# A new order for the first tiles' attention, joined with reworked token mixing

## Chip, cores and metric

The kernel runs on one core of a Trainium2 chip. The metric is the device time of one execution in microseconds (us). TensorE is called PE in the profile (PEld is its weight load), VectorE is DVE, ScalarE is ACT, GpSimd is POOL, SyncE is SP.

## What is computed

```
attn = softmax(mask(q @ k.T / 8)) @ v            # 4 batches, 8 heads, 576 tokens, 64 per head; window of 64 keys
x    = attn as [4, 576, 512]
xn   = (x - mean) / sqrt(var + 1e-6) * g
x    = x + relu(xn @ wa1) @ wa2                  # 512 -> 2048 -> 512
h    = relu(x.T @ tok1) @ tok2                   # token mixing, 576 -> 256 -> 576, over the tokens
u    = x + h.T
out  = u + relu(u @ wb1) @ wb2                   # 512 -> 1536 -> 512
```

All inputs are fp32. The weights come in as 64-bit words and are turned into fp32 on the chip, and each large product is made of three passes, since each operand is split into a high and a low part (`PASSES` in line 339).

## The kernel before, in words

The 2304 tokens are 18 tiles of 128, in six blocks of three tiles. There are four stages.

**Opening.** Ten matmuls on zeros (line 391) run while the first loads are under way. Then the attention of the first three tiles runs by a list written out by hand, `FIRST` (line 39), one letter and number for each step; the same list sets the order on all engines, since each engine takes its instructions in program order. `S` t makes the scores of tile t on PE (line 181) and takes the mask, the scale and the row maximum on DVE (line 192; half a tile has the number u = 2t or 2t+1). `e` u is the exponential on ACT with the row sum as a second output (line 200). `T` u and `U` u transpose the probabilities on PE (line 213) and copy them out of PSUM on ACT (T, line 217) or on DVE (U, line 215), and they invert the row sums: on POOL in two instructions after a T (lines 219, 220), on DVE in two after a U (lines 222, 223). `V` u multiplies with v on PE (line 265) and by the inverse sum on DVE (line 267). `L` takes mean and variance on DVE (lines 273, 274) and the root on POOL, `N` subtracts the mean on DVE (line 292), `X` and `Y` transpose the result on PE (line 302), `E` c leaves chunk c in `xnt`, its high part by ACT (line 319) and its low part by DVE (line 320). `D` n are n filler matmuls. `k`, `n` and `s` turn a piece of weights: `k` shrinks it on ACT (line 101), `n` narrows it on DVE in two instructions (lines 111 and 114), `s` splits it into a high part (ACT, line 93) and a low part (POOL, line 94) and loads the next piece on ACT's queue (line 427).

The row sums of each half tile have a tile with the tag `sm`, of which there are four buffers (line 190), so the fifth half tile's waits for the first one to be used by `V`. Loads of q, k, v go by SP's queue, first q and k of tile 0, then in the order of `LOADS` (line 48): v0, q and k of tile 1, v1, the gains, q and k of tile 2, v2, and six pieces of weights.

**Blocks a.** Six blocks, each 16 steps f: 12 matmuls of 384 columns (line 353), relu and split (ACT line 342, DVE line 343), and 9 matmuls of 512 columns for step f-2 (line 366). Hooks put the attention of the next block between them. In the first block the hooks also turn two pieces of weights a step: `wnarrow(2)` runs line 111 for both pieces and then line 114 for both, ahead of the relu; `wsplit` comes behind it. In the last block there is no attention, and 13 pieces of the later weights are turned (`b_narrow`, `b_split`).

**Token mixing.** `tok_up` (line 698) runs four times, with two groups of 14 matmuls each: 13 with 128 rows, and as the last one 64 rows of the rest of the tokens, `(w_[r, 1], y[r])` in line 710. `tok_down` (line 717) runs once for each of the 18 tiles, 6 matmuls each (12 for tiles 8 and 17) into one of three PSUM buffers, and DVE adds the result to the tile (line 731). Tiles 0 to 8 come after the first two `tok_up`, 9 to 17 after the other two. Between the steps DVE makes `ut`, the transposed first block, in 16 block transposes (line 328, list `parts`): eight in `tok_up(2)`, eight in `tok_up(3)`. `b_conv` turns one piece of weights: after `tok_up(2)` and after tiles 11, 13 and 15.

**Blocks b.** Six blocks of 12 steps, the same two matmul lines. In the first of them each step turns one piece of weights, so the pieces used last are turned last.

Of the kernel before, what the change touches and what calls it, by code (L numbers as in the profile page):

```python
# [35 lines left out]

FIRST = ("S0 e0 e1 S1 e2 T0 U1 e3 S2 V0 V1 L0 e4 T2 U3 e5 N0 X0 V2 V3 L1 T4 U5 k1 N1 X1 V4 V5 L2 n1 D10 N2 X2 Y0 "
         "k1 D4 s0 n1 E0 E1 E2 E3 s0 k2")  # L40


WARM = 10
# [1 line left out]

LAG = 2

LOADS = ("v0 q1 v1 g0 q2 v2 w6")


def tile_blocks(t):
# [9 lines left out]
def mixer_kernel(ctx, tc, qT, kT, v, g, wa1, wa2, tok1, tok2, wb1, wb2, out):  # L61
# [18 lines left out]
    masks = const.tile([P, 2, 2 * BLK], BF16, name="masks")  # L80
    gsb = const.tile([P, KD], F32, name="gsb")
    mhalf = const.tile([P, 1], F32, name="mhalf")
    mone = const.tile([P, 1], F32, name="mone")
    qkv = const.tile([P, 3, 2, DM], F32, name="qkv")

    def wslot(k, shape, name, dtype=F32R):
# [13 lines left out]
        h_ = raw.rearrange("p (n two) -> p n two", two=2)[:, :, 1].bitcast(F32)  # L100
        nc.scalar.activation(out=h_, in_=h_, func=AF.Prelu, scale=2.0 ** -112, alpha=2.0 ** 32)

    def narrow(pairs, steps=(0, 1)):

        for step in steps:
            for d, r in pairs:
                w = r.rearrange("p (n two) -> p n two", two=2)
                if step == 0:  # L110
                    nc.vector.tensor_scalar(out=d, in0=w[:, :, 0], scalar1=29, scalar2=None,
                                            op0=ALU.logical_shift_right)
                else:
                    nc.vector.scalar_tensor_tensor(out=d, in0=w[:, :, 1], scalar=3, in1=d,
                                                   op0=ALU.logical_shift_left, op1=ALU.bitwise_or)
        return [d.bitcast(F32) for d, _ in pairs]


# [11 lines left out]
    def place_fixed(t):  # L130
        place_in(t, qkv[:, 0, 0], qkv[:, 1], qkv[:, 2])

    def load_qk(t):
        (ba, ia), (bb, ib) = tile_blocks(t)
        ga, gb = ba * NBLK + ia, bb * NBLK + ib
        if ba == bb:
            nc.sync.dma_start(out=Q[t], in_=qT[:, ga:ga + 2, :])
            first = 1 if ia == 0 else 0
            nc.sync.dma_start(out=K[t][:, first:3], in_=kT[:, ga - 1 + first:ga + 2, :])
        else:  # L140
            for s, g_ in ((0, ga), (1, gb)):
                nc.sync.dma_start(out=Q[t][:, s], in_=qT[:, g_, :])
                nc.sync.dma_start(out=K[t][:, 2 * s:2 * s + 2], in_=kT[:, g_ - 1:g_ + 1, :])
# [18 lines left out]
    def att_S(t, lean, first=False):  # L162


        (ba, ia), (bb, _) = tile_blocks(t)
        m_ = masks[:, 1 if ia == 0 else 0]
        wide = [P, NH, 2 * BLK]
        s_ = [ps_acc.tile(wide, F32, tag="acc", name=f"s{2 * t + hh}") if first else
              ps_a.tile(wide, F32, tag="a", name=f"s{2 * t + hh}") for hh in range(2)]
        for h in range(NH):  # L170
            c = slice(h * BLK, (h + 1) * BLK)
            for hh in range(2):
                r = slice(64 * hh, 64 * hh + 64)
                for s in range(2):
                    if s == 0 and ia == 0:

                        k_ = K[t][r, 1:2, c].to_broadcast([64, 2, BLK])
                    else:
                        j = s if ba == bb else 2 * s
                        k_ = K[t][r, j:j + 2, c]  # L180
                    nc.tensor.matmul(s_[hh][64 * s:64 * s + 64, h], lhsT=Q[t][r, s, c], rhs=k_, start=True, stop=True)  # L181
        for hh in range(2):
            u = 2 * t + hh
            if first:
                f_ = scratch[:, u]
            else:
                f_ = sp.tile(wide, F32, tag="s", name=f"f{u}") if lean else whole[t][:, hh]
            probs[u] = f_
            mx = peak[u] = stp.tile([P, NH, 1], F32, tag="mx", name=f"mx{u}")
            norm[u] = stp.tile([P, NH, 1], F32, tag="sm", bufs=4, name=f"sm{u}") if lean else sums[t][:, hh]  # L190
            for h in range(NH):
                nc.vector.tensor_tensor_reduce(out=f_[:, h], in0=s_[hh][:, h], in1=m_, scale=-(D ** -0.5),  # L192
                                               scalar=-2.0 * MASK, op0=ALU.add, op1=ALU.min, accum_out=mx[:, h])
            if lean and not first:
                att_E(u)
# [7 lines left out]
    def att_T(u, first=False, copy=None):  # L203
        f_, sm = probs.pop(u), norm[u]
        if first:
            p_ = ps_h.tile([P, NH, P], F32, tag="h", name=f"pt{u}")
            s_ = hp.tile([P, 2 * N], F32, tag="hT", name=f"pts{u}")[:, 0:NH * P].rearrange("p (h c) -> p h c", h=NH)
        else:
            p_ = ps_a.tile([P, NH, P], F32, tag="a", name=f"pt{u}")
            s_ = sp.tile([P, NH, P], F32, tag="s", name=f"pts{u}")  # L210
        probsT[u] = s_
        for h in range(NH):
            nc.tensor.transpose(p_[:, h, :], f_[:, h, :], ident)
        if copy:
            copy(out=s_, in_=p_)
        else:
            nc.scalar.activation(out=s_, in_=p_, func=AF.Copy)
        if first and not copy:
            nc.gpsimd.tensor_scalar_add(out=sm, in0=sm, scalar1=SM_EPS)
            nc.gpsimd.tensor_tensor(out=sm, in0=sm, in1=mone.unsqueeze(1).to_broadcast([P, NH, 1]), op=ALU.pow)  # L220
        else:
            nc.vector.tensor_scalar_add(out=sm, in0=sm, scalar1=SM_EPS)
            nc.vector.reciprocal(out=sm, in_=sm)

    whole, wholeT, sums = {}, {}, {}

# [8 lines left out]
    def tile_T_part(t, n):  # L235

        if n == 0:
            wholeT[t] = ap.tile([P, 2, NH, P], F32, tag="p", name=f"pts{t}")
        f_, s_ = (x[t].rearrange("p two h c -> p (two h) c") for x in (whole, wholeT))
        a, b = divmod(n, 4)  # L240
        nc.vector.transpose(out=s_[32 * b:32 * b + 32, :, 32 * a:32 * a + 32],  # L241
                            in_=f_[32 * a:32 * a + 32, :, 32 * b:32 * b + 32])
        if n == 15:
            del whole[t]
            for hh in range(2):
                probsT[2 * t + hh] = wholeT[t][:, hh]
            sm = sums.pop(t)
            nc.vector.tensor_scalar_add(out=sm, in0=sm, scalar1=SM_EPS)
            nc.vector.reciprocal(out=sm, in_=sm)

    def tile_PV(t):
        del wholeT[t]
# [132 lines left out]
    with tc.manual_schedule():  # L385
# [10 lines left out]
            place_in(t, qs[:, t - 1, 0], kv_[:, 0], kv_[:, 1])  # L396
        for t in range(TPB):
            new_x(t)
        load_qk(0)

        make_identity(nc, ident)
        for i in (1, 0):
# [9 lines left out]
                nc.gpsimd.memset(m_[0:64, 0], MASK)  # L412
            nc.vector.tensor_copy(out=masks[:, i], in_=m_.rearrange("p s c -> p (s c)"))
        nc.gpsimd.memset(mhalf, -0.5)
        nc.gpsimd.memset(mone, -1.0)
# [50 lines left out]
        def first_X(j, c):  # L466
# [1 line left out]

        fns = {"S": lambda t: att_S(t, True, True), "e": att_E, "D": dummies, "T": lambda u: att_T(u, True),
               "U": lambda u: att_T(u, True, nc.vector.tensor_copy), "V": att_PV,  # L470
               "L": ln_stats, "N": ln_center, "k": wshrink, "n": wnarrow, "s": lambda _: wsplit(False),
               "X": lambda j: [first_X(j, c) for c in range(KD - 1)],
               "Y": lambda _: [first_X(j, KD - 1) for j in range(TPB)], "E": lambda c: evac(c)}
        scratch = xnp.tile([P, 2 * TPB, NH, P], F32, tag="xn", name="scratch")
# [89 lines left out]
                    shrink(x[2][:, 0:2 * x[3]])  # L564
                    x[0] = True

        def b_narrow(n=1):
            b_shrink(n)
            pairs = []
            for _, k, raw, width, parts in ready_b[:n]:  # L570
                tmp = sp.tile([P, DM], U32, tag="s", name=f"tmpb{k}")
                pairs.append((tmp[:, 0:width], raw[:, 0:2 * width]))
                rawb.append(raw)
            narrowed_b.extend((parts, w) for (_, _, _, _, parts), w in zip(ready_b[:n], narrow(pairs)))
# [10 lines left out]
        def b_conv(n=1):  # L585
            for _ in range(n):
                b_narrow()
                b_split()

# [108 lines left out]
        def tok_up(b, between=()):  # L698
            pr, o = divmod(b, 2)
            hb = h1[b] = wslot((12, 13, 14, 13)[b], [P, 2, 2, DM], f"h1_{b}")  # L700
            r = slice(64 * o, 64 * o + 64)
            for tt in range(2):
                ts = slice(tt * P, (tt + 1) * P)
                p_ = ps_h.tile([P, DM], F32, tag="h", name=f"th{b}_{tt}")
# [2 lines left out]
                    w_, y = tw["t1"][:, :, j, ts], ysl(9 * pr + 4 * o + j)  # L707
                    ops += [(w_[:, a], y[:, c]) for a, c in PASSES]
                w_, y = t2[0][:, :, 704 + tt * P:704 + (tt + 1) * P], ysl(9 * pr + 8)[:, o]
                ops += [(w_[:, 0], y), (w_[r, 1], y[r])]  # L710
                for n, (a, b) in enumerate(ops):
                    nc.tensor.matmul(p_, lhsT=a, rhs=b, start=n == 0, stop=n == len(ops) - 1)  # L712
                relu_split(hb[:, tt, 0], hb[:, tt, 1], p_)
# [24 lines left out]
        for t in range(9):  # L738
            tok_down(t)
            if t < 5:  # L740
                new_ys(1, t)
                for y in range(9 + 2 * t, min(11 + 2 * t, 18)):
                    y_split(y, nc.gpsimd if y < 17 else None)
            else:
                y_rest_low(17, t - 5)
        tok_up(2, parts[:8])
        b_conv()
        tok_up(3, parts[8:])
        for c in range(KD):
            split(xnt[:, c, 0], xnt[:, c, 1], ut[:, c], nc.gpsimd)  # L750
        b_shrink()
        for t in range(9, 18):
            tok_down(t)
            if t in (11, 13, 15):
                b_conv()


# [89 lines left out]
```

## Time and profile before

| what | us |
|---|---|
| median of 3 runs (lowest, highest) | 844.45 (843.27, 845.39) |
| the profiled execution, its own time | 844.72 |
| its span, first to last instruction | 842.6 |
| PE busy / DVE / ACT / POOL in the span | 824.9 / 524.5 / 282.0 / 119.5 |
| mean granted clock of PE | 0.996 |

The span is what the trace shows; the 2.1 us beside it are before the first and after the last instruction. Busy time of PE is modelled from pipelined matmuls, so a busy PE need not be at its peak: the question for each stretch is how long the same number of matmuls takes there and elsewhere.

### The profile page before, as it was taken

What the parts mean: (1) busy time and instruction counts of PE and PEld (TensorE: products, weight loads), DVE (VectorE), ACT (ScalarE), POOL (GpSimd) and SP (SyncE); (2) the same over time, 40 slices, a digit from 0 to 9 for tenths busy, and PEclk for the clock granted to TensorE, in tenths of its full rate; (3) what the DMA queues carried; (4) which work ended last, traced back from release to release, by engine and by line L of the source; (5) the groups of instructions that cost most, each with busy time, mean ns of one, the idle gap of its engine ahead of it and who ended that gap; (6) DMA issues with size and microseconds to landing.
All of it is one profiled execution on the core that took longest, in us unless ns stands there. A gap on an engine that the chain in (4) does not pass through costs nothing.

```text
span 842.6 us, 13017 instructions
## 1 busy us (share of the span) xinstructions
PE 824.9 (98%) x5022; PEld 728.8 (86%) x5022; DVE 524.5 (62%) x1313; ACT 282.0 (33%) x759; POOL 119.5 (14%) x141
## 2 busy tenths in 40 slices
PE   6899999999999999999999999999999999999997
PEld 5788888888888888889999876898999999899996
DVE  4899868777787878678557557975343434344211
ACT  5577543334324333442245332432111111111110
POOL 3555510000000000000005341532000000000000
PEclk8999999999999999999999999999999999999999
DMA  9577302102100110211006400531001010010101
GB/s 327 185 264 269 137 32 77 38 26 88 58 26 26 57 57 26 96 58 43 1 0 195 124 1 25 200 100 38 1 0 39 1 38 1 1 37 1 38 1 37
DMA packets 23213, 58.37 MB, mean 69 GB/s; under 512 B 2800, under 2 KB 3568, under 8 KB 23152
## 3 DMA queue, kind: packets, MB, share of 16 engines
q1 hardware_dynamic: 19408, 43.92, 15.7%
q10 hardware_dynamic: 3744, 13.63, 4.5%
q8 instruction: 39, 0.64, 0.3%
q14 instruction: 22, 0.18, 0.1%
HBM read 52.82 MB, written 4.72 MB: 68 GB/s over the span
## 4 chain that ended last, share of the span: by engine, by line
PE 90%; DVE 3%; issue 1%; ACT 1%; POOL 0%; DVEq 0%; ACTq 0%
PE acca L366 23%; PE ha L353 23%; PE hb L353 18%; PE accb L366 17%; PE td L728 2%; PE o L265 2%; PE s L181 2%; PE th L712 1%; DVE ut L328 1%; PE king_offset=None)_1_4976 L712 0%; PE king_offset=None)_1_5121 L712 0%; PE king_offset=None)_1_4941 L712 0%; DVE us L94 0%; DVE xs L731 0%; DVE xs L799 0%
## 5 line engine op out<-in xcount | busy, mean ns | idle before, releaser
L353 PE MATMUL ha<-xnt,wa 128*128 128x384 f32 x1152 | 217.4, 337 | 1.3 <-DVE xnt L320 0.7
L366 PE MATMUL acca<-wa,hTa 128*128 128x512 f32 x864 | 215.9, 396 | 0.0
L353 PEld LDWEIGHTS ha<-xnt,wa 128*128 128x128 f32 x1152 | 203.7, 188 | 9.9 <-DVE xnt L320 1.0
L366 PEld LDWEIGHTS acca<-wa,hTa 128*128 128x128 f32 x864 | 159.0, 188 | 32.5 <-issue 1.7
L366 PE MATMUL accb<-wb,hTb 128*128 128x512 f32 x648 | 159.1, 392 | 0.0
L366 PEld LDWEIGHTS accb<-wb,hTb 128*128 128x128 f32 x648 | 120.7, 188 | 22.5
L343 DVE SCALAR_TENSOR_TENSOR hTb<-hb,hTb 128x384 fp32r<-128x384 f32 x72 | 40.1, 557 | 150.3 <-ACT hTb L342 150.2
L342 ACT ACTIVATE hTb<-hb 128x384 fp32r<-128x384 f32 x72 | 35.4, 492 | 238.6 <-PE hb L353 238.6
L342 ACT ACTIVATE hTa<-ha 128x384 fp32r<-128x384 f32 x96 | 46.6, 486 | 180.4 <-PE ha L353 180.3
L343 DVE SCALAR_TENSOR_TENSOR hTa<-ha,hTa 128x384 fp32r<-128x384 f32 x96 | 53.1, 553 | 85.8 <-ACT hTa L342 84.3
L241 DVE STREAM_TRANSPOSE pts<-f 32x256 f32<-32x256 f32 x192 | 83.6, 436 | 2.8
L353 PE MATMUL hb<-xnt,wb 128*128 128x384 f32 x432 | 80.9, 337 | 1.1 <-POOL wb L94 0.7
L353 PE MATMUL hb<-us,wb 128*128 128x384 f32 x432 | 80.5, 336 | 0.0
L353 PEld LDWEIGHTS hb<-xnt,wb 128*128 128x128 f32 x432 | 76.4, 188 | 4.4 <-POOL wb L94 1.1
L353 PEld LDWEIGHTS hb<-us,wb 128*128 128x128 f32 x432 | 76.5, 188 | 2.6
L336 DVE STREAM_TRANSPOSE xhT<-xh 32x128 f32<-32x128 f32 x192 | 57.9, 302 | 3.1
L200 ACT ACTIVATE f<-f,mx 128x128 f32<-128x128 f32 x120 | 46.5, 389 | 29.4 <-DVE mx L192 29.4
L328 DVE STREAM_TRANSPOSE ut<-xs 32x384 f32<-32x384 f32 x96 | 54.6, 569 | 1.9
L94 POOL TENSOR_TENSOR wa<-tmp,wa 128x512 fp32r<-128x512 f32 x32 | 42.2, 1339 | 34.6 <-ACT wa L93 34.6
L286 POOL TENSOR_SCALAR mv<-mv 128x1 f32<-128x1 f32 x12 | 2.3, 191 | 276.5 <-ACT xhT L285 276.5
L94 POOL TENSOR_TENSOR wb<-tmpb,wb 128x512 fp32r<-128x512 f32 x24 | 32.9, 1380 | 53.9 <-ACT wb L93 53.9
L728 PE MATMUL td<-h,t 128*128 128x512 f32 x120 | 28.6, 395 | 1.6 <-DVE xs L731 1.6
(113 smaller groups left out, 682.4 us busy)
## 6 DMA issues: line engine op xcount, KB each, us to landing
xs<-in_wa ACTq DMA_DIRECT2D x26, 512.0 KB, 4.3
qkv<-in_wb SPq DMA_DIRECT2D x20, 512.0 KB, 4.2
qkv<-in_v SPq DMA_DIRECT2D x28, 256.0 KB, 2.8
out<-xs SPq DMA_DIRECT2D x16, 256.0 KB, 2.1
qkv<-in_kT SPq DMA_DIRECT2D x10, 384.0 KB, 3.3
qkv<-in_qT SPq DMA_DIRECT2D x14, 256.0 KB, 2.7
xs<-in_wa SPq DMA_DIRECT2D x6, 512.0 KB, 7.8
qkv<-in_kT SPq DMA_DIRECT2D x8, 256.0 KB, 3.3
```

The lines of the kernel that those rows point to most:

```text
L94: lo_engine.tensor_tensor(out=dst_lo, in0=src, in1=dst_hi.bitcast(F32), op=ALU.subtract)
L181: nc.tensor.matmul(s_[hh][64 * s:64 * s + 64, h], lhsT=Q[t][r, s, c], rhs=k_, start=True, stop=True)
L200: nc.scalar.activation(out=f_[:, h], in_=f_[:, h], func=AF.Exp, scale=-1.0, bias=mx[:, h], accum_out=sm[:, h])
L241: nc.vector.transpose(out=s_[32 * b:32 * b + 32, :, 32 * a:32 * a + 32], in_=f_[32 * a:32 * a + 32, :, 32 * b:32 * b + 32])
L265: nc.tensor.matmul(o_[r, h], lhsT=p_[:, h, r], rhs=v_[:, s, hh * NH + h, :], start=True, stop=True)
L328: nc.vector.transpose(out=d_[:, :, :, 32 * a:32 * a + 32], in_=s_[:, :, :, 32 * b:32 * b + 32])
L336: nc.vector.transpose(out=uts[t][32 * b:32 * b + 32, :, 32 * a:32 * a + 32], in_=s_)
L342: nc.scalar.activation(out=dst_hi, in_=src, func=AF.Relu)
L343: nc.vector.scalar_tensor_tensor(out=dst_lo, in0=src, scalar=0.0, in1=dst_hi.bitcast(F32), op0=ALU.max, op1=ALU.subtract)
L353: nc.tensor.matmul(h_, lhsT=w[:, a, cs], rhs=src[c][:, b], start=n == 0, stop=n == 3 * KD - 1)
L366: nc.tensor.matmul(acc[j], lhsT=t_[:, a, js], rhs=w[:, 2 + b, :], start=f == 0 and n == 0, stop=f == F - 1 and n == 2)
L728: nc.tensor.matmul(p_, lhsT=t2[tt][:, a, col:col + P], rhs=h1[b][:, tt, c], start=n == 0, stop=n == last)
```

## The change

The opening's list has a new order and no `U5`, `L1` and `N1`: half tile 5 is copied by ACT (`T5`), and tile 1 has its mean and variance taken on ACT in three activations and POOL in two instructions (`l1`). A new step `r` t inverts the sums of a whole tile on DVE in two instructions; neither T nor U inverts any more in the opening, and the sums of the first three tiles lie in a tile of their own each. q and k of tile 1 are loaded ahead of v0, q and k of tile 2 ahead of v1, and the keys of tile 0 go by ACT's queue. `narrow` runs both its instructions for one piece before the next piece's; for the later weights (`b_narrow`) the value between them lies in PSUM instead of SBUF. In the token mixing the last matmul of a group has all 128 rows; two block transposes each run behind tiles 3 and 4; `b_conv` runs inside `tok_up(3)` and once more, behind tile 16.

```diff
-FIRST = ("S0 e0 e1 S1 e2 T0 U1 e3 S2 V0 V1 L0 e4 T2 U3 e5 N0 X0 V2 V3 L1 T4 U5 k1 N1 X1 V4 V5 L2 n1 D10 N2 X2 Y0 "
-         "k1 D4 s0 n1 E0 E1 E2 E3 s0 k2")
+FIRST = ("S0 e0 e1 S1 T0 r0 U1 e2 V0 V1 S2 L0 e3 T2 r1 U3 e4 V2 V3 N0 X0 e5 T4 r2 T5 k1 V4 l1 V5 D6 L2 X1 n1 N2 k1 "
+         "s0 n1 X2 Y0 D4 E0 E1 E2 E3 s0 k2")
-LOADS = ("v0 q1 v1 g0 q2 v2 w6")
+LOADS = ("q1 v0 q2 v1 g0 v2 w6")
-    def narrow(pairs, steps=(0, 1)):
+    def narrow(pairs, pool=None):
+        for d, r in pairs:
+            w, low = r.rearrange("p (n two) -> p n two", two=2), d
+            if pool:
+                low = pool.tile([P, DM], U32, tag="acc" if pool is ps_acc else "a", name="low")[:, 0:d.shape[1]]
+            nc.vector.tensor_scalar(out=low, in0=w[:, :, 0], scalar1=29, scalar2=None, op0=ALU.logical_shift_right)
+            nc.vector.scalar_tensor_tensor(out=d, in0=w[:, :, 1], scalar=3, in1=low,
+                                           op0=ALU.logical_shift_left, op1=ALU.bitwise_or)
...
-            nc.sync.dma_start(out=K[t][:, first:3], in_=kT[:, ga - 1 + first:ga + 2, :])
+            eng.dma_start(out=K[t][:, first:3], in_=kT[:, ga - 1 + first:ga + 2, :])
...
-            norm[u] = stp.tile([P, NH, 1], F32, tag="sm", bufs=4, name=f"sm{u}") if lean else sums[t][:, hh]
+            if first and hh == 0:
+                sums[t] = stp.tile([P, 2, NH, 1], F32, tag="sums", name=f"sums{t}")
+            norm[u] = sums[t][:, hh] if first or not lean else stp.tile([P, NH, 1], F32, tag="sm", bufs=4, name=f"sm{u}")
...
-        if first and not copy:
-            nc.gpsimd.tensor_scalar_add(out=sm, in0=sm, scalar1=SM_EPS)
-            nc.gpsimd.tensor_tensor(out=sm, in0=sm, in1=mone.unsqueeze(1).to_broadcast([P, NH, 1]), op=ALU.pow)
-        else:
-            nc.vector.tensor_scalar_add(out=sm, in0=sm, scalar1=SM_EPS)
-            nc.vector.reciprocal(out=sm, in_=sm)
+        if not first:
+            inverse(sm)
+    def inverse(sm):
+        nc.vector.tensor_scalar_add(out=sm, in0=sm, scalar1=SM_EPS)
+        nc.vector.reciprocal(out=sm, in_=sm)
...
-        load_qk(0)
+        load_qk(0, nc.scalar)
...
-               "L": ln_stats, "N": ln_center, "k": wshrink, "n": wnarrow, "s": lambda _: wsplit(False),
+               "L": ln_stats, "l": ln_scalar, "r": lambda t: inverse(sums.pop(t)), "N": ln_center, "k": wshrink, "n": wnarrow, "s": lambda _: wsplit(False),
...
-        def b_narrow(n=1):
+        def b_narrow(n=1, pool=ps_a):
...
+        def b_conv():
+            b_narrow(1, ps_acc)
+            b_split()
...
-                ops += [(w_[:, 0], y), (w_[r, 1], y[r])]
+                ops += [(w_[:, a], y) for a in range(2)]
...
+            if t in (3, 4):
+                for fn in parts[:2]:
+                    fn()
+                del parts[:2]
         tok_up(2, parts[:8])
-        b_conv()
-        tok_up(3, parts[8:])
+        tok_up(3, [b_conv, *parts[8:], lambda: None, lambda: None, lambda: None])
...
-            if t in (11, 13, 15):
+            if t in (11, 13, 15, 16):
                 b_conv()
```

## Rows read from the trace of the kernel before

**Rows 1.** The page: the chain that ended last, shares of the span by engine.

```profile
PE 90%; DVE 3%; issue 1%; ACT 1%; POOL 0%; DVEq 0%; ACTq 0%
```

**Rows 2.** Stretches: us, then PE, PEld, DVE, ACT, POOL busy; PE clock; DMA share; GB/s.

```profile
7.30:31.46 24.16, 17.04 (x225) 14.61 (x225) 17.17 (x76) 14.44 (x58) 8.13 (x13) 0.86 0.74 275
36.00:60.00 24.00, 22.81 (x194) 19.47 (x193) 23.15 (x49) 17.77 (x44) 14.01 (x11) 1.00 0.78 264
```

**Rows 3.** Groups of DVE, 7.2 to 31.4 us: busy us, mean ns | idle before, releasers.

```profile
L192 DVE CUSTOM_DVE_ANT_0 scratch<-s,masks 128x128 f32<-128x128 f32 x24 | 5.3, 286 | 5.4 <-PE s L181 2.9 <-ACT scratch L200 2.5
L267 DVE TENSOR_TENSOR xs<-o,sm 128x256 f32<-128x256 f32 x6 | 2.4, 422 | 3.1 <-PE o L265 3.1
L114 DVE SCALAR_TENSOR_TENSOR tmp<-xs,tmp 128x512 uint32<-128x512 uint32 x2 | 2.4, 1208 | 0.2
L273 DVE BATCH_NORM_STATS2 st<-xs 128x6 f32<-128x512 f32 x3 | 2.1, 695 | 0.1
L215 DVE COPY pts<-pt 128x512 f32<-128x512 f32 x3 | 2.0, 680 | 0.7 <-PE pt L213 0.7
...
L292 DVE TENSOR_SCALAR xh<-xs,mv 128x512 f32<-128x512 f32 x3 | 1.4, 468 | 0.0
L111 DVE TENSOR_SCALAR tmp<-xs 128x512 uint32<-128x512 uint32 x2 | 0.8, 407 | 0.0
```

**Rows 4.** Timeline of the opening: start us, us, engine, line [idle before <-releaser].

```profile
1.31 4.64 PE L391 MATMUL idle<-zero 128*128 128x512 f32 x10 [1.31 <-POOL zero L388]
...
5.88 1.41 PE L181 MATMUL s<-qkv 64*64 64x128 f32 x32
...
9.71 2.00 PE L181 MATMUL s<-kv,q 64*64 64x128 f32 x32 [2.42 <-DMA kv<-in_kT]
...
16.84 0.40 ACT L200 ACTIVATE scratch<-scratch,mx 128x128 f32<-128x128 f32 x1 [1.24 <-DVE xs L267]
...
31.46 2.18 DVE L320 SCALAR_TENSOR_TENSOR xnt<-tpa,gsb,xnt 128x384 fp32r<-128x384 f32 x4
```

**Rows 5.** Timeline of the token mixing and the start of block b, PE and PEld.

```profile
480.60 2.79 PEld L712 LDWEIGHTS king_offset=None)_1_4941<-ys,t 128*128 128x128 f32 x13 [0.25 <-issue]
...
484.17 2.79 PEld L712 LDWEIGHTS th<-ys,t 128*128 128x128 f32 x13 [0.24 <-issue]
...
491.38 13.94 PE L728 MATMUL td<-h,t 128*128 128x512 f32 x60
...
519.39 4.42 PE L728 MATMUL td<-h,t 128*128 128x512 f32 x18
...
525.24 7.23 PE L728 MATMUL td<-h,t 128*128 128x512 f32 x30 [1.43 <-DVE xs L731]
...
535.54 6.43 PE L353 MATMUL hb<-xnt,wb 128*128 128x384 f32 x36
```

**Rows 6.** Timeline of DVE around the second nine tiles of the token mixing.

```profile
522.13 2.33 DVE L328 STREAM_TRANSPOSE ut<-xs 32x384 f32<-32x384 f32 x4
524.49 1.89 DVE L731 TENSOR_TENSOR xs<-td,xs 128x512 f32<-128x512 f32 x3
...
527.41 1.39 DVE L114 SCALAR_TENSOR_TENSOR tmpb<-qkv,tmpb 128x512 uint32<-128x512 uint32 x1
```

**Rows 7.** Timeline of PE at the last steps of the first block b.

```profile
575.29 2.25 PE L366 MATMUL accb<-wb,hTb 128*128 128x512 f32 x9
...
579.28 2.03 PE L353 MATMUL hb<-xnt,wb 128*128 128x384 f32 x10 [0.73 <-POOL wb L94]
581.14 6.32 PE L366 MATMUL accb<-wb,hTb 128*128 128x512 f32 x27
```

**Rows 8.** Beside each other in the first block a; then the page's group of line 343.

```profile
85.30 2.98 POOL L94 TENSOR_TENSOR wa<-tmp,wa 128x512 fp32r<-128x512 f32 x2 [2.35 <-ACT wa L93]
...
85.61 2.96 DVE L111 TENSOR_SCALAR tmp<-xs 128x512 uint32<-128x512 uint32 x2
...
L343 DVE SCALAR_TENSOR_TENSOR hTa<-ha,hTa 128x384 fp32r<-128x384 f32 x96 | 53.1, 553 | 85.8 <-ACT hTa L342 84.3
```

More of the change, by code (lines that the diff above doesn't have):

```diff
@@ L82, in mixer_kernel @@
     mhalf = const.tile([P, 1], F32, name="mhalf")
-    mone = const.tile([P, 1], F32, name="mone")
     qkv = const.tile([P, 3, 2, DM], F32, name="qkv")
@@ L101, in shrink @@
         nc.scalar.activation(out=h_, in_=h_, func=AF.Prelu, scale=2.0 ** -112, alpha=2.0 ** 32)
-    def narrow(pairs, steps=(0, 1)):
[L107 to L112, printed above, removed]
-                else:
-                    nc.vector.scalar_tensor_tensor(out=d, in0=w[:, :, 1], scalar=3, in1=d,
-                                                   op0=ALU.logical_shift_left, op1=ALU.bitwise_or)
+    def narrow(pairs, pool=None):
[6 more added lines that the diff above has]
+                                           op0=ALU.logical_shift_left, op1=ALU.bitwise_or)
         return [d.bitcast(F32) for d, _ in pairs]
@@ L131, in place_fixed, with load_qk @@
         place_in(t, qkv[:, 0, 0], qkv[:, 1], qkv[:, 2])
-    def load_qk(t):
+    def load_qk(t, eng=nc.sync):
         (ba, ia), (bb, ib) = tile_blocks(t)
@@ L217, in att_T @@
             nc.scalar.activation(out=s_, in_=p_, func=AF.Copy)
-        if first and not copy:
-            nc.gpsimd.tensor_scalar_add(out=sm, in0=sm, scalar1=SM_EPS)
-            nc.gpsimd.tensor_tensor(out=sm, in0=sm, in1=mone.unsqueeze(1).to_broadcast([P, NH, 1]), op=ALU.pow)
-        else:
-            nc.vector.tensor_scalar_add(out=sm, in0=sm, scalar1=SM_EPS)
-            nc.vector.reciprocal(out=sm, in_=sm)
+        if not first:
[3 more added lines that the diff above has]
+        nc.vector.reciprocal(out=sm, in_=sm)
     whole, wholeT, sums = {}, {}, {}
@@ L246, in tile_T_part @@
                 probsT[2 * t + hh] = wholeT[t][:, hh]
-            sm = sums.pop(t)
-            nc.vector.tensor_scalar_add(out=sm, in0=sm, scalar1=SM_EPS)
-            nc.vector.reciprocal(out=sm, in_=sm)
+            inverse(sums.pop(t))
     def tile_PV(t):
@@ L414, in mixer_kernel @@
         nc.gpsimd.memset(mhalf, -0.5)
-        nc.gpsimd.memset(mone, -1.0)
         warm = stp.tile([P, NH, 1], F32, tag="mx", name="warm")[:, 0]
@@ L573, in b_narrow @@
                 rawb.append(raw)
-            narrowed_b.extend((parts, w) for (_, _, _, _, parts), w in zip(ready_b[:n], narrow(pairs)))
+            narrowed_b.extend((parts, w) for (_, _, _, _, parts), w in zip(ready_b[:n], narrow(pairs, pool)))
             del ready_b[:n]
@@ L583, in b_split @@
             del narrowed_b[:]
[L585 to L588, printed above, removed]
+        def b_conv():
+            b_narrow(1, ps_acc)
+            b_split()
         STEPS = ("S0", "T0*7", "T0*8", "T0*1 S1", "V0 T1*3", "T1*8", "T1*5 X0*4", "S2 X0*2", "V1 X0*5", "T2*8",
@@ L700, in tok_up @@
             hb = h1[b] = wslot((12, 13, 14, 13)[b], [P, 2, 2, DM], f"h1_{b}")
-            r = slice(64 * o, 64 * o + 64)
             for tt in range(2):
```

## The prediction, as it was made before the changed kernel ran

> **What bounds it now.** I read the chain of work first: 90% of it is PE [rows 1], so the kernel ends when PE has done its matmuls, and whatever lets PE start its steady work sooner, or closes a hole in it, comes off the end one for one. Then I looked for the places where PE is not in steady work, by the timeline of each stretch, and found three that the change touches. The opening: PE has little to do until DVE writes the low part of the first chunk of `xnt` at 31.46 [rows 4], since the first block needs it. From 7.30 to there DVE is busy 17.17 of 24.16 us, against ACT's 14.44, and PE's granted clock is 0.86 on average: at two levels, 1.2 and 2.4 GHz, some 28% of that stretch ran at the lower one [rows 2]. DVE's idle 7.0 us are waits for the first products, in series with PE and ACT [rows 3]. The token mixing: its groups take longer than their matmuls, and PE stands once for 1.43 us for DVE [rows 5]. The end of the first block b: PE stands for weights that POOL has not yet split [rows 7].
>
> The sum is made against the profiled execution, 844.72 us (span 842.6, and 2.1 around it). The median of the three runs lies 0.27 lower; I don't correct for that. Less than 0.3%, 2.5 us, a measurement of this kernel can't tell from no change.
>
> **The opening.** I take DVE's queue from the end of the first scores, 5.88 + 1.41 = 7.29, since DVE sets the end.
>
> The first scores don't move. They start as the ten warm-up matmuls end, at 1.31 + 4.64 = 5.95 [rows 4], so the keys by a second queue bring nothing there, nor cost anything: SP issues one load less.
>
> The second tile's scores wait 2.42 us for its keys [rows 4], which stood seventh on SP and now stand third. PE then waits for something else: three PSUM buffers hold scores, and the fourth half tile's needs the first one read by DVE, about 1 us after 7.29 (four of the 24 reductions of 0.29). So about 1.4 of 2.42 is gained, and the second reductions run almost at once; v0, behind three loads more, is not wanted until two transposes are copied. The wait of 1.24 for the multiply of V0 before the fifth exponential [rows 4] goes: it was for a buffer of row sums, and each tile has its own now.
>
> Work leaves DVE: one statistic (0.695), one copy (0.680), one subtraction (0.468) [rows 3], 1.8 us. The inverses on DVE stay three pairs; those on POOL go, and were waited for by no one. ACT gets one copy and three activations for tile 1, about 2.7 us at the copy's 0.68 for 512 columns; it was busy 14.44 of 24.16 [rows 2], and it sits beside V4, V5 and the narrowing. The second narrowing's L114 took about 1.7: the mean of the two is 1208 ns, and 0.7 is its length alone by the copy of as many columns, 680 ns [rows 3]. POOL was splitting beside it; now the subtraction N2 and the shrink stand between, and POOL starts later against it: 1.0 gained, or nothing.
>
> Of the 7.0 idle us I count through the new order: 0.4 before the second reductions, 0.4 at U1 and V1, 0.6 before the third ones, 0.3 at V3, 2.3 while X0, T4, T5 and V4 run in series behind N0, 0.9 elsewhere, 4.9 together. That gains 2.1. Sum 1.8 + 1.0 + 2.1 = 4.9. If the clock falls again while T4, T5, V4 and V5 run, they take some 1.3 us more (an estimate: about 2.3 us of work in series, at half the speed, a part of it behind ACT); PE's holes are shorter than before, but V3 and X0 still wait about 2 and 1 us. I take off 0.5 for that: **4.4 us gained**, between 2.0 (the work alone) and 6.0. What comes next, the first block, keeps its order and moves with it: its loads go out from the splits, so none has a fixed time.
>
> **Narrowing.** Both instructions for one piece, then for the next: the same four. The first piece is ready one L111 earlier, and POOL starts sooner, beside the second piece's two. In the first block DVE is the tight engine, 23.15 of 24 us [rows 2]. I take 0, between 1 gained and 3 lost, by L111's 0.407 alone [rows 3] and 2.96 for two beside POOL [rows 8].
>
> **Token groups.** Two groups of 14 matmuls start 484.17 - 480.60 = 3.57 apart by their weight loads; 60 whole matmuls of the same width take 13.94 less 0.16 of overlap, 0.230 each, so 14 would take 3.22 [rows 5]. The 0.35 is the 64-row matmul, before and behind which PE's loads stop. With 128 rows it is like the other 13; the added products come from rows that are loaded anyway. Eight groups: **2.75 gained**, between 2.4 and 2.85.
>
> **Second nine tiles.** From 519.39 to 535.54 they take 16.15 against 13.78 for the same 60 matmuls in the first nine: 2.37 lost, 1.43 in one wait [rows 5]. It begins with DVE's backlog: eight transposes stand ahead of the adds, the last four from 522.13 to 524.46 [rows 6]. Four of the 16 now run behind tiles 3 and 4: each pair is 1.15 there, DVE falls behind by at most about 1 us, and PE has three buffers of 1.38 us, so no hole. Behind `tok_up(3)` the adds start some 2.5 us after the tiles do, ahead of the fourth tile's need at 4.1. Five conversions in place of four now stand in DVE's queue, at twice 0.7 each if PSUM keeps them free of POOL, by the copy out of PSUM [rows 3]. The nearest rows for an instruction with one operand in PSUM are those of line 343: 553 ns in the mean of 96, most of them beside POOL [rows 8]; against that L114 took 1.39 there with both in SBUF [rows 6]. I take the first: DVE then has nine adds of 0.63 (three in 1.89), four conversions of 1.4 and 1.3 of backlog, 12.6 us in 13.8. **2.1 gained**, between 1.0 and 2.4.
>
> The Trainium skill, "SBUF — State Buffer", "Who interferes with whom", says that a DVE instruction with two SBUF inputs, or in a two-port mode, locks GpSimd out or waits for its whole instruction, and that one with at most one SBUF input outside such a mode does neither. By that rule the narrowing through PSUM costs DVE its bare length, and by it the first block's narrowing, which stays in SBUF, is open to the loss in the third rival.
>
> **First block b.** From 575.29 to 581.14 are 5.85 us for 9 and 12 matmuls that take 9 x 0.230 + 12 x 0.174 = 4.16 (0.174 from 36 in 6.43 - 0.16) [rows 5, 7]: 1.7 lost, since the last step's weights were split as it began. With a fifth conversion in the token mixing each piece comes one step, over 4 us, earlier, more than the hole. **1.7 gained**, at worst 0.8. The later narrowings through PSUM in the last block a have slack around them: 0.
>
> **Sum:** 4.4 + 0 + 2.75 + 2.1 + 1.7 = 10.95, so 844.7 - 10.9 = **833.8 us**.
>
> **Rivals.**
> First, the opening gives little: T4, T5, V4 and V5 behind X0 run at the low clock, and three activations of tile 1 on ACT hold the split that the first block needs. For it: 28% at low clock before, and N0 stands at the end of DVE's queue as before. Against it: DVE's work is less whatever PE does. It would gain 1 instead of 4.4: 837.2.
>
> Second, DVE stays behind in the second nine tiles. It was busy nearly all the time there, and gets one conversion more; if L111 and L114 still wait for POOL, each conversion costs some 1.4 more (0.7 for L114, and I put as much for L111), four of them 5.6, and the 2.1 gain turns into a loss of about 2: 838. Against it are line 343's lengths.
>
> Third, slower: the first block. If each step's second L111 or L114 finds POOL in its first split, which the old order kept behind all four, DVE waits out one split of 1.28 (two in 2.98, less a wait for one L111 of 0.41) [rows 8]. In 16 steps that is 20 us. From about 0.4 us a step DVE, with 0.85 us free in 24 [rows 2], holds up PE; were later steps to absorb 6, 14 would stay, 844.7 - 10.9 + 14 = 848. Against it: in the rows shown the old order has both L111 waiting for POOL in many steps, so one collision takes another's place.
>
> That a part does nothing is in the forecast for the second queue; the 64-row matmul can't but go.
>
> **Chances.** The forecast 0.70, the first rival 0.15, the second 0.09, the third 0.06. The range: low, all upper bounds, 6.0 + 1 + 2.85 + 2.4 + 1.7 = 14, to 831; the rivals reach to 838, and both together with 1 us lost in the first block to 840. I give 830.5 to 840. Faster by over 0.3% are the forecast and the first two rivals and a mild third, 0.92; within 0.3% 0.04, where the third takes about as much as is gained; slower 0.04.
>
> **What would show it.** Right: the low part of the first chunk at about 27 us in place of 31.46; no 64-row loads, and token groups 3.2 us apart; the second nine tiles in about 14 us with no wait for line 731; L111 near 0.6 and L114 near 0.69 with POOL beside them; no wait for POOL at the end of the first block b. Wrong: most of the first block's second L111 or L114 over 1.3 us, with PE idle where DVE is tight; the clock at 0.5 around 20 us; or a first block that takes longer than before from its first low part to its last matmul, which would say that the opening's gain was given back.

## The result, and the profile after

| | before | after |
|---|---|---|
| median of 4 runs each, us (lowest, highest) | 844.28 (843.27, 845.39) | 833.48 (833.0, 833.97) |
| the profiled execution, its own time | 844.72 | 833.0 |
| its span | 842.6 | 830.8 |
| mean granted clock of PE | 0.996 | 0.999 |

The ratio is 0.9876 with the interval 0.9863 to 0.9888. The kernel after is faster by 1.24%. The forecast was 833.8; the sum of its terms, 10.95, stands against 10.80 between the medians.

The two profiled executions lie 11.72 us apart, 0.9 more than the medians: the first lies 0.44 above its median, the second 0.48 below. The last section returns to that. To see where the 11.72 lie, take one place of PE's stream that both kernels have, and subtract. The first is the twelve matmuls of the first block's third step, from which PE works steadily.

PE in the timeline of the kernel before: start, us, engine, line, operation, tiles, shapes, count.

```profile
37.38 2.35 PE L353 MATMUL ha<-xnt,wa 128*128 128x384 f32 x12
...
112.94 2.27 PE L353 MATMUL ha<-xnt,wa 128*128 128x384 f32 x12
...
477.14 3.54 PE L712 MATMUL th<-ys,t 128*128 128x512 f32 x14
...
505.15 3.54 PE L712 MATMUL th<-ys,t 128*128 128x512 f32 x14
...
587.30 6.43 PE L353 MATMUL hb<-us,wb 128*128 128x384 f32 x36
```

The same places of the kernel after, and those between them (its lines are numbered a little lower).

```profile
32.91 2.35 PE L350 MATMUL ha<-xnt,wa 128*128 128x384 f32 x12
...
108.69 2.27 PE L350 MATMUL ha<-xnt,wa 128*128 128x384 f32 x12
...
472.88 3.34 PE L706 MATMUL th<-ys,t 128*128 128x512 f32 x14
...
485.57 13.76 PE L722 MATMUL td<-h,t 128*128 128x512 f32 x60
...
499.17 3.33 PE L706 MATMUL th<-ys,t 128*128 128x512 f32 x14
...
511.87 13.76 PE L722 MATMUL td<-h,t 128*128 128x512 f32 x60
...
525.47 6.43 PE L350 MATMUL hb<-xnt,wb 128*128 128x384 f32 x36
...
575.57 6.43 PE L350 MATMUL hb<-us,wb 128*128 128x384 f32 x36
```

| stage | before | after | gained | forecast |
|---|---|---|---|---|
| opening, to the third step | 37.38 | 32.91 | 4.47 | 4.4 |
| first block a, from there to the next block | 75.56 | 75.78 | -0.22 | 0 |
| token groups (64-row matmul) | | | 3.44 | 2.75 |
| second nine tiles, the hole | 16.15 | 13.60 | 2.37 (2.55 less 0.18 counted above) | 2.1 |
| first block b | 51.76 | 50.10 | 1.66 | 1.7 |

The token groups' 3.44 is two things: the two `tok_up` ahead of each nine tiles took 14.24 and take 12.69 and 12.70, and each nine tiles take 13.60. The first nine took 13.77 before, and the second nine would have taken 13.78 without their hole, as they do in the run with 64 rows below. The stages between gave nothing (0.01), and the sum is 11.72.

**The opening** now looks like this. The first row answers to [rows 2], the rest to [rows 4].

Stretch of the kernel after, from 7.30 to the first low part: us, then PE, PEld, DVE, ACT, POOL busy; PE clock; DMA share; GB/s.

```profile
7.30:25.72 18.42, 13.04 (x209) 10.63 (x208) 14.04 (x72) 15.95 (x62) 2.57 (x5) 1.00 0.88 335
```

Timeline of the kernel after.

```profile
5.87 1.30 PE L178 MATMUL s<-qkv 64*64 64x128 f32 x32
...
8.29 1.09 PE L178 MATMUL s<-kv,q 64*64 64x128 f32 x28 [0.91 <-DVE mx L191]
...
20.57 1.17 PE L262 MATMUL o<-kv,pts 128*64 128x64 f32 x32 [0.25 <-ACT pts L216]
...
25.11 0.69 DVE L111 SCALAR_TENSOR_TENSOR tmp<-xs,tmp 128x512 uint32<-128x512 uint32 x1
25.72 2.19 DVE L317 SCALAR_TENSOR_TENSOR xnt<-tpa,gsb,xnt 128x384 fp32r<-128x384 f32 x4
...
26.50 2.54 POOL L93 TENSOR_TENSOR wa<-tmp,wa 128x512 fp32r<-128x512 f32 x2
...
27.84 4.11 PE L350 MATMUL ha<-xnt,wa 128*128 128x384 f32 x22 [0.99 <-POOL wa L93]
```

The reader is to see three things. The first low part starts at 25.72 in place of 31.46, 5.74 earlier. Of these DVE's busy time gives 17.17 - 14.04 = 3.13, and its idle time (24.16 - 17.17) - (18.42 - 14.04) = 2.61. The granted clock is 1.00 all through, where it was 0.86. And the next to be late is POOL: its split of the first weights begins at 26.50, PE waits 0.99 us for it, and of 5.74 us only 4.47 reach the third step.

**The narrowing.** Groups of DVE on the page of the kernel after: busy us, mean ns | idle before. The first two go through PSUM, the last two stay in SBUF.

```profile
L111 DVE SCALAR_TENSOR_TENSOR tmpb<-qkv,low 128x512 uint32<-128x512 uint32 x24 | 16.5, 688 | 2.9
L110 DVE TENSOR_SCALAR low<-qkv 128x512 uint32<-128x512 uint32 x24 | 16.5, 686 | 0.9 <-DMA qkv<-in_tok 0.5 <-DMA qkv<-in_wb 0.3
...
L111 DVE SCALAR_TENSOR_TENSOR tmp<-xs,tmp 128x512 uint32<-128x512 uint32 x32 | 26.9, 840 | 3.9 <-ACT xs L100 0.9
L110 DVE TENSOR_SCALAR tmp<-xs 128x512 uint32<-128x512 uint32 x32 | 22.5, 702 | 0.0
```

### The profile page after: what moved, and what is told of

It reads as the page before. It is cut to its first block, busy times and chain, and to the rows that moved or that the text cites. A ratio compares the mean times of both kernels' runs of the same rounds, so it can differ in the third digit from the quotient of the medians.

```text
span 830.8 us, 12970 instructions
## 1 busy us (share of the span) xinstructions
PE 817.2 (98%) x5014; PEld 726.7 (87%) x5014; DVE 512.4 (62%) x1309; ACT 284.5 (34%) x765; POOL 115.8 (14%) x134
## 4 chain that ended last, share of the span: by engine, by line
PE 93%; DVE 1%; ACT 0%; issue 0%; ACTq 0%; DVEq 0%
PE acca L363 24%; PE ha L350 23%; PE hb L350 18%; PE accb L363 18%; PE td L722 3%; PE o L262 2%; PE s L178 2%; PE th L706 2%; DVE tmp L111 1%; PE king_offset=None)_1_5123 L706 0%; PE king_offset=None)_1_5174 L706 0%; PE king_offset=None)_1_4974 L706 0%; PE king_offset=None)_1_4939 L706 0%; DVE xs L796 0%; DVE tmp L110 0%; PE pt L212 0%
## 5 line engine op out<-in xcount | busy, mean ns | idle before, releaser
L93 POOL TENSOR_TENSOR wa<-tmp,wa 128x512 fp32r<-128x512 f32 x32 | 45.2, 1432 | 30.2 <-ACT wa L92 30.2
L93 POOL TENSOR_TENSOR wb<-tmpb,wb 128x512 fp32r<-128x512 f32 x24 | 31.0, 1297 | 51.8 <-ACT wb L92 51.8
L111 DVE SCALAR_TENSOR_TENSOR tmp<-xs,tmp 128x512 uint32<-128x512 uint32 x32 | 26.9, 840 | 3.9 <-ACT xs L100 0.9
```

The lines of the kernel that those rows point to most:

```text
L93: lo_engine.tensor_tensor(out=dst_lo, in0=src, in1=dst_hi.bitcast(F32), op=ALU.subtract)
```

## The experiments

Most take one part back from the kernel after; the one that holds the clock is an edit of the kernel before, and the last one tries a further step. Each was run once, with a profile, but the last, which was run four times. One time says little below 1 us, so the verdicts come from the stages of each trace.

**64 rows again.**

```diff
-                ops += [(w_[:, a], y) for a in range(2)]
+                ops += [(w_[:, 0], y), (w_[r, 1], y[r])]
```

> The changed kernel with the last matmul of a token group on 64 rows again. If the 64-row matmul is what stretched the groups, they start 3.5 to 3.6 us apart again instead of 3.17, and the token mixing (from its first group to the first matmul of block b, 52.6 us in the changed kernel) takes 55.5 to 55.9. If the stretch came from the turn to a new PSUM buffer, the groups stay at 3.2 and the stage at 52.6.

It took 836.92. Its token mixing:

```profile
473.13 3.54 PE L707 MATMUL th<-ys,t 128*128 128x512 f32 x14
...
487.37 13.94 PE L723 MATMUL td<-h,t 128*128 128x512 f32 x60
...
529.16 6.43 PE L350 MATMUL hb<-xnt,wb 128*128 128x384 f32 x36
```

From 473.13 to 529.16 are 56.03, against 52.59 after (55.5 to 55.9 was expected): 3.44, all that the table puts down to this part. The 60 matmuls of nine tiles take 13.94 again, and 13.76 in the kernel after, though no line of them was changed. The trace shows where: the 64-row matmul starts at 486.95 and the first of the tiles at 487.37, 0.42 later, the second 0.34 behind that, and only after some ten are they 0.227 apart, as they are from the first one on in the kernel after.

**The narrowing through SBUF again.**

```diff
-            if pool:
+            if False:
```

> The changed kernel with the narrowed low bits of the later weights left in SBUF instead of PSUM. If waiting for POOL is what PSUM takes away, L110 and L111 of the later weights are 0.42 and 0.69 us alone and 1.1 to 1.9 beside POOL, DVE falls behind in the second nine tiles and they take 14.5 to 16 us instead of 13.6, with a wait of PE for line 725. If the moved transposes alone closed the hole, they stay at 13.6 to 13.8 us.

834.59. The second instruction got longer, but the time was lost elsewhere than expected: the second nine tiles kept their 13.60 (512.20 to 525.80), and PE then waited at the start of block b. Page, and timeline:

```profile
L111 DVE SCALAR_TENSOR_TENSOR tmpb<-qkv,tmpb 128x512 uint32<-128x512 uint32 x24 | 23.9, 995 | 2.5 <-ACT qkv L100 0.4
```

```profile
531.20 2.37 PE L350 MATMUL hb<-xnt,wb 128*128 128x384 f32 x12 [1.05 <-DVE hTb L340]
...
577.25 6.43 PE L350 MATMUL hb<-us,wb 128*128 128x384 f32 x36
```

L111 takes 995 ns in place of 688, and the first block b 51.45 in place of 50.10. So PSUM is worth some 1.35 us, in that block. The Trainium skill, "SBUF — State Buffer", "Who interferes with whom", has it that a DVE instruction with two SBUF inputs contends with a GpSimd instruction that reads SBUF, and that one with at most one SBUF input, outside the two-port modes, doesn't. The trace agrees for L111, 995 against 688 ns beside the same splits. For L110, with one input, nothing is gained in the mean: 684 ns in SBUF, 686 through PSUM. But in SBUF it is 0.42 us (at 510.46) or 1.29 (at 520.14), and through PSUM 0.69 and 0.68 at the same places (510.13 and 519.70 in the kernel after). Whether it is in a two-port mode in SBUF no run here shows.

**All 16 block transposes behind the token groups again.**

```diff
-            if t in (3, 4):
-                for fn in parts[:2]:
-                    fn()
-                del parts[:2]
...
-        tok_up(3, [b_conv, *parts[8:], lambda: None, lambda: None, lambda: None])
+        tok_up(3, [b_conv, *parts[8:12], *parts[12:], lambda: None])
```

> The changed kernel with all 16 block transposes behind the token groups again (none behind tiles 3 and 4). If DVE's backlog of transposes made the hole, the second nine tiles take 14.0 to 15.5 us instead of 13.6. If the cheaper conversions did it, they stay at 13.6.

835.5. Timeline:

```profile
512.13 4.24 PE L722 MATMUL td<-h,t 128*128 128x512 f32 x18
...
518.05 9.83 PE L722 MATMUL td<-h,t 128*128 128x512 f32 x42 [1.67 <-DVE xs L725]
527.72 6.43 PE L350 MATMUL hb<-xnt,wb 128*128 128x384 f32 x36
```

The hole is back, at the same place as in [rows 5]: 15.59 us (14.0 to 15.5 was expected), 1.99 lost, of the 2.37 before. The four transposes moved forward are what closes most of it.

**No conversion behind tile 16.**

```diff
-            if t in (11, 13, 15, 16):
+            if t in (11, 13, 15):
```

> The changed kernel without the conversion behind tile 16. If the piece that comes one step earlier closed the hole at the end of the first block b, PE waits there for POOL again and that block takes 51.5 to 51.9 us instead of 50.1, the second nine tiles staying at 13.6. If the narrowing through PSUM is what closed it, the block stays at 50.1 to 50.4.

835.99. Timeline:

```profile
526.17 6.43 PE L350 MATMUL hb<-xnt,wb 128*128 128x384 f32 x36
...
568.89 0.62 PE L350 MATMUL hb<-xnt,wb 128*128 128x384 f32 x2 [0.71 <-ACT wb L92]
...
570.25 2.02 PE L350 MATMUL hb<-xnt,wb 128*128 128x384 f32 x10 [0.74 <-POOL wb L93]
...
578.27 6.43 PE L350 MATMUL hb<-us,wb 128*128 128x384 f32 x36
```

The first block b takes 52.10, 2.0 more (51.5 to 51.9 was expected), and its last steps wait for their weights as in [rows 7]. The fifth conversion is what removes that, and it costs the second nine tiles nothing.

**The keys of tile 0 on SP, and the old order of loads.**

```diff
-        load_qk(0, nc.scalar)
+        load_qk(0)
```

> The changed kernel with the keys of tile 0 on SP's queue again, all other loads in the new order. By the prediction the first scores start when the warm-up matmuls end, at 5.9, on either queue; SP's later loads go out 0.45 us later, and the first matmuls of block a's third step (32.9 to 33.3 us in the changed kernel and its variants) start within 0.3 us of that. If two queues matter, the second tile's scores and all behind them come 0.5 us later or more.

```diff
-LOADS = ("q1 v0 q2 v1 g0 v2 w6")
+LOADS = ("v0 q1 v1 g0 q2 v2 w6")
```

> The changed kernel with the old order of loads (v0 ahead of q and k of tile 1, v1 ahead of those of tile 2), keys of tile 0 on ACT's queue. If the keys' place in the queue is worth what the prediction put on it, the second tile's scores start at 9.2 to 9.4 us instead of 8.3, PE stands longer ahead of them, and the third step of block a starts 0.7 to 2.0 us later, more if the granted clock falls to half again. If the exponentials of tile 0 on ACT hide it, it starts within 0.3 us of 33.

833.63 and 835.1. Timeline of the one with the keys on SP:

```profile
5.87 1.77 PE L178 MATMUL s<-qkv 64*64 64x128 f32 x32
...
8.59 1.26 PE L178 MATMUL s<-kv,q 64*64 64x128 f32 x32 [0.95 <-DMA kv<-in_kT]
...
33.37 2.35 PE L350 MATMUL ha<-xnt,wa 128*128 128x384 f32 x12
```

Timeline of the one with the old order of loads:

```profile
9.06 1.22 PE L178 MATMUL s<-kv,q 64*64 64x128 f32 x32 [1.77 <-DMA kv<-in_kT]
...
34.79 2.35 PE L350 MATMUL ha<-xnt,wa 128*128 128x384 f32 x12
```

With one queue the second scores wait for the keys of tile 1, and end at 9.85 in place of 9.38; the third step is 0.46 later. That doesn't show that the second queue is worth 0.47, since the first scores took 1.77 in this run and 1.30 in the kernel after, which is the same 0.47. The run with the sums one by one (below) has both queues and first scores as long:

```profile
5.88 1.78 PE L178 MATMUL s<-qkv 64*64 64x128 f32 x32
...
8.78 1.09 PE L178 MATMUL s<-kv,q 64*64 64x128 f32 x28 [0.91 <-DVE mx L189]
```

There PE waits for the first reductions in place of the keys, and the second scores end at 9.87. The keys do come later with one queue, which moves them back one place on SP: at 8.59, against 6.85 to 8.06 in five runs with two queues and the same order of loads in which PE stood for them. Here that time lay beside another wait; in a run with short first scores it might not, and that was not tried.

With the old order of loads the second scores end at 10.28, 0.4 to 0.9 later than in the six runs with the new order whose first scores began at 5.87 or 5.88 (9.38 to 9.87). The third step comes 1.88 later than in the kernel after; 1.0 of that lies behind the second scores, and the clock fell in that run (below).

**Copy, statistics and subtraction on DVE again.** Only `FIRST` is changed.

```diff
-... T4 r2 T5 k1 V4 l1 V5 D6 L2 X1 n1 N2 k1 ...
+... T4 r2 U5 k1 L1 V4 N1 V5 D6 L2 X1 n1 N2 k1 ...
```

> The changed kernel with the copy of half tile 5, the statistics and the centring of tile 1 on DVE again (U5, L1, N1 for T5, l1). If work that leaves DVE is gained in full, the third step of block a starts 1.5 to 2.0 us later than 33. If DVE waits for PE and ACT there anyway (it stands idle for about 2 us ahead of the product of tile 2), the work fits into the wait, and the step starts within 0.5 us of 33, or earlier, since ACT has four instructions less.

**The old order of the steps,** with the new loads, sums, copy and statistics:

```diff
-S0 e0 e1 S1 T0 r0 U1 e2 V0 V1 S2 L0 e3 T2 r1 U3 e4 V2 V3 N0 X0 e5 T4 r2 T5 k1 V4 ...
+S0 e0 e1 S1 e2 T0 r0 U1 e3 S2 V0 V1 L0 e4 T2 r1 U3 e5 N0 X0 V2 V3 T4 r2 T5 k1 V4 ...
```

> The changed kernel with the steps of the opening in the order of before (third exponential ahead of the first transpose, third scores ahead of the first products, sixth exponential ahead of the centring), but with the new loads, sums and the copy and statistics on ACT. If the order is what shortens DVE's waits, the third step of block a starts 0.7 to 2.0 us later than 33. If loads and moved work did it, it starts within 0.5 us of 33.

834.69 and 833.24. Timeline of the one with the work on DVE:

```profile
5.21 1.10 PE L178 MATMUL s<-qkv 64*64 64x128 f32 x32
...
7.67 1.25 PE L178 MATMUL s<-kv,q 64*64 64x128 f32 x32 [1.35 <-DMA kv<-in_kT]
...
34.10 2.35 PE L350 MATMUL ha<-xnt,wa 128*128 128x384 f32 x12
```

Timeline of the one with the old order of the steps:

```profile
7.26 1.25 PE L178 MATMUL s<-kv,q 64*64 64x128 f32 x32 [0.95 <-DMA kv<-in_kT]
...
32.60 2.35 PE L350 MATMUL ha<-xnt,wa 128*128 128x384 f32 x12
```

The old order reaches the third step at 32.60, before the new one's 32.91. That is a miss: the order up to `T4`, which is what was put back, gives nothing in this run. What comes behind `T4`, the splits ahead of `X2` for one, stayed as in the kernel after; no run put that back. The work on DVE costs 34.10 - 32.91 = 1.19, or less: both runs started their scores 0.66 early and had the clock fall later, so they stand better beside the runs of that kind (below). With the work on DVE the second L111 also runs beside POOL's split again: it takes 1.72 (at 26.55) in place of 0.69.

**The sums one by one,** in four rotating buffers, inverted by half tiles:

```diff
-            norm[u] = sums[t][:, hh] if first or not lean else ...
+            norm[u] = sums[t][:, hh] if not lean else ...
-"r": lambda t: inverse(sums.pop(t)),
+"r": lambda t: [inverse(norm[2 * t + hh]) for hh in range(2)],
```

> The changed kernel with the row sums of each half tile in the four rotating buffers again, inverted one half tile after the other (two small DVE instructions more a tile). If the buffer was still short in the new order, the fifth exponential waits for the first product's multiply and the third step of block a starts 0.5 us or more later after the first scores than 27.0. By the new order that multiply ends at 12.4 us and the fifth exponential starts at 14.9, so I expect no wait, and 0 to 0.4 us for the six instructions.

834.0; third step at 33.90. The fifth exponential, whose wait of 1.24 [rows 4] I had put down to the four buffers, did not wait here: in the new order the multiplies come before it. What it costs is six small DVE instructions more, about 0.5 us, a little over the 0.4 expected (24.03 from the end of the second scores to the third step, against 9.38 to 32.91, 23.53, in the kernel after).

**The clock held in the kernel before,** by filler matmuls:

```diff
-S0 e0 e1 S1 ... U3 e5 ...
+S0 e0 e1 D18 S1 ... U3 D20 e5 ...
```

> The kernel before with 18 filler matmuls behind the first scores and 20 behind the transposes of tile 1, where PE stands for more than 2 us; nothing else is changed. If the half clock that follows those stands costs time of its own, PE's clock is 1.0 from 7 to 25 us and the third step of block a starts 30.0 to 30.8 us after the first scores instead of 31.5 (27.0 in the changed kernel). If DVE sets the end whatever PE's clock is, it starts within 0.3 us of 31.5.

845.89, and no answer. The fillers, two instructions each in the trace, took 4.29 and 4.63 us, more than the holes that they were to fill. The clock was 1.0 throughout, yet from the second scores' end to the third step are 25.97 us against 25.67.

**The first block's narrowing step by step again.**

```diff
+        if not pool:
+            for step in (0, 1):
+                for d, r in pairs:
+                    ...
```

> The changed kernel with the first block's narrowing step by step again (line 110 for both pieces, then line 111 for both). From the third step of block a to the first of the second block it takes 75.8 us in the changed kernel and 75.6 in the one before. By the prediction's zero, 75.4 to 76.0. If the new order brings collisions of line 111 with POOL that cost PE time, 74.5 or less.

833.59. Timeline, then a stretch with columns as above:

```profile
5.68 1.10 PE L189 MATMUL s<-qkv 64*64 64x128 f32 x32
...
20.57 1.98 PE L273 MATMUL o<-kv,pts 128*64 128x64 f32 x32
...
33.38 2.35 PE L361 MATMUL ha<-xnt,wa 128*128 128x384 f32 x12
...
108.95 2.27 PE L361 MATMUL ha<-xnt,wa 128*128 128x384 f32 x12
```

```profile
18.50:22.00 3.50, 3.49 (x37) 3.16 (x39) 0.49 (x3) 1.92 (x4) 0.00 (x0) 0.58 1.03 393
```

The block takes 75.57, as before (75.56), and 75.76 to 76.06 in the kernel after and the nine other runs that leave that block as it is there: piece by piece costs 0.2 to 0.5 there, no more. Its opening has the same order as that of the kernel after, yet the clock is 0.58 from 18.5 to 22, and the last multiply with v takes 1.98 us where it took 1.17.

**The roots of tiles 1 and 2 later on POOL,** behind the first two splits. Of the edit only the list is shown; the roots got a step `R` of their own.

```diff
-... E3 s0 k2
+... E3 s0 R1 R2 k2
```

> The changed kernel with POOL's four instructions for the roots of tiles 1 and 2 behind the first two splits of weights instead of ahead of them. In the changed kernel ACT has split the first piece's high part by 24.9 us, and POOL starts its low part at 26.5, behind those four; PE then stands 0.99 us for it. If they are what holds the split, that wait goes, the third step of block a starts 0.5 to 1.0 us earlier after the first scores than 27.0, and the kernel takes about 832.8 us where the changed one takes 833.5. If DVE's low parts of the chunks come last anyway, it starts within 0.2 us of 27.0.

835.03 (834.65 to 835.14); the ratio to the kernel before is 0.9884 (0.9868 to 0.9900), so it does not beat the kernel after. Timeline:

```profile
25.42 1.27 POOL L93 TENSOR_TENSOR wa<-tmp,wa 128x512 fp32r<-128x512 f32 x1 [7.70 <-ACT wa L92]
25.52 1.73 DVE L111 SCALAR_TENSOR_TENSOR tmp<-xs,tmp 128x512 uint32<-128x512 uint32 x1
...
27.83 4.30 PE L355 MATMUL ha<-xnt,wa 128*128 128x384 f32 x23 [0.75 <-DVE xnt L322]
...
44.63 2.01 PE L355 MATMUL ha<-xnt,wa 128*128 128x384 f32 x10 [0.81 <-POOL wa L93]
...
110.45 2.27 PE L355 MATMUL ha<-xnt,wa 128*128 128x384 f32 x12
```

POOL's split starts 1.08 earlier, and the wait for POOL is gone. But L111 now finds it running and takes 1.73 in place of 0.69; PE waits 0.75 for DVE at the same moment, 27.83. The third step is 0.18 later (0.22 earlier, counted from the end of the second scores, which came at 9.78 here), and the first block 77.36 long, 1.58 more, with a wait of 0.81 for POOL in it. So in the kernel after the four small root instructions are what keeps POOL off DVE's narrowing.

## Why the prediction was right, point by point

**Second tile's keys.** Forecast 1.4 us earlier, measured 9.71 - 8.29 = 1.42; what comes next is the first reductions, 0.91 (line 191), as said. That the keys of tile 0 by a second queue bring nothing was forecast for the first scores. Without it the keys of tile 1 come later, which I had not looked at, but no run shows that this costs time.

**Idle time by the new order.** The count itself came out in the kernel after, item by item: 0.34 before the second reductions (0.4 forecast), 0.37 at V1 (0.4), 0.57 before the third ones (0.6), 0.46 at V3 (0.3), 2.14 while T4, T5 and V4 run (2.3), 4.38 together (4.9), and so 2.61 less than before in place of 2.1. The step that failed is the reason, "through the new order": with the old one as far as `T4`, the third step comes no later. From the second scores' end it takes 24.09 with the old order, and 24.39 to 24.70 in three runs with the new one whose clock fell likewise.

What the runs show in its place is the keys and the clock. In the kernel before the second scores took 2.00 us [rows 4], the clock being 0.57 while they ran, and as many matmuls take 1.22 to 1.26 at full rate: about 0.75. Later, from V3's matmuls to the fillers D6, six runs with this part of the new order take 4.38 at full rate, and five whose clock fell there 5.58 to 5.62. These 1.2 are the "1.3 more" of the prediction. Of them 0.9 to 1.2 reach the third step: 23.51 to 23.53 from the second scores' end in the kernel after and two runs at full rate (64 rows, block transposes), 24.39 to 24.70 in the three with the same opening whose clock fell (SBUF, no conversion, step by step). I had taken 0.5 off for a clock that falls again; in the timed profile it did not fall. What remains, no run separates: the sums' own tiles, the inverses off POOL, for which [rows 3] shows no wait, and the order behind `T4`.

**Work off DVE.** 1.8 forecast. Beside the runs whose clock fell likewise, putting it back makes the first low part 1.7 later (19.28 from the second scores' end, against 17.53 to 17.56), and of that 1.03 is L111's collision with POOL, the next point. So the work itself is worth some 0.7, less than half; the rest lay beside other waits. At the third step both together are 25.18 - 24.4 to 24.7 = 0.5 to 0.8, since PE's wait for POOL went. That is one run.

**L114's collision.** The 1.0 is right in size: two took 2.42 [rows 3], now 2 x 0.693. The reason was wrong: not the subtraction and the shrink, but the roots on POOL keep the split late, as the last experiment shows. The root of tile 1 comes late because ACT makes its statistics: with these on DVE again, the collision was back (1.72).

**What I left out.** The opening's gain on DVE, 5.74, is larger than the sum of these terms; 1.27 of it stays at the wait for POOL's split, which the sum did not have. Two omissions of opposite sign left 4.47 beside 4.4. That closeness is luck, the more so as the clock fell in the one profile and not in the other.

**Narrowing in the first block.** 0 forecast, -0.22 measured; taken back, the block took 75.57: a small loss, within the bound of 3. The third rival's 20 us of collisions did not come: L111's mean there is 840 ns, 0.15 us above that through PSUM.

**Token groups.** The mechanism stood, the size was short: 3.44 for 2.75, beyond the upper bound of 2.85. The mis-sized term is the base, "0.230 each": it was taken from nine tiles that the 64-row matmuls had lengthened by 0.17. At 13.60 / 60 = 0.2267 fourteen take 3.17, a group loses 0.386, and eight 3.09; the two times 0.17 make the rest. They are what the last 64-row matmul does to those behind it, as the starts in the first experiment show.

**Second nine tiles.** 2.1 forecast, 2.37 measured, no wait left. Each instruction takes 0.69, as taken from the copy (line 343's 553 ns, on which the choice also leaned, are for 384 columns). But that is not why five conversions fit: in SBUF they fit, too. The second rival needed the collisions with POOL at 1.4 a conversion; in SBUF they come back, at some 0.6 (four conversions take 7.78 there and 5.49 through PSUM), and DVE's lateness then shows in block b and not in the tiles.

**First block b.** 1.7 forecast, 1.66 measured, and 2.0 lost where the fifth conversion is left out, so the mechanism stood.

## What to carry to other kernels

Measure the price of an odd-shaped instruction against a stretch that has none of it, since it also slows what follows. When two runs differ by half a microsecond in a stretch, look at the runs whose edit doesn't touch that stretch: here their first scores differed by as much. And when an engine is relieved, look at once for who is late next: here POOL's split, 1 us behind DVE, and starting it earlier only moved the collision.

## What the runs showed of the hardware

The same opening has two outcomes. In the kernel after the first scores begin at 5.87, as the warm-up ends, and PE's granted clock is 1.00 from 7.30 to the first low part. In the run with the first block's narrowing step by step, whose opening has the same order, they begin at 5.68, and the clock is 0.58 from 18.5 to 22: of the two levels 1.2 and 2.4 GHz mostly the lower. Before it fell, PE stood twice, 1.58 us for the copy U3 and 0.92 for N0, and it stood just as long in the kernel after, 0.40 us later in the span, where nothing fell. The other early starters (5.20 to 5.60 in four runs) had a mean of 0.90 from 7.3 to 25 too; of the kernel after and its variants that started at 5.87 or 5.88 only the one with the old order of loads did. Third steps of otherwise equal openings lie between 32.9 and 33.4, so one trace tells the place of this opening's end to some 0.25 us.

The kernel before varies more. In its profile the clock falls twice, both times in the opening (0.57 while the second scores ran, 9.71 to 11.71, and 0.74 from 18.5 to 22). Nine further runs of it have spans of 841.5 to 844.4 us at mean granted clocks of 0.998 to 0.991, the longest at the lowest; the profiled one, 842.6 at 0.996, lies between. So the opening's 4.47 holds for this pair of runs. If those spans differ in the opening alone, which their clocks suggest and no trace of them shows, other runs of the kernel before would make it from 1.1 less to 1.8 more. What decides between the two outcomes is open; no run tried it.
